# Gated linear attention with routed experts: late tiles routed in pairs, and each expert's weights split beside other products

## The chip, the cores and the metric

The kernel runs on one core of a Trainium2 chip, as one program. The metric is the time of an execution on the device in microseconds (us), as the median of three runs. Matrix products run on TensorE (PE), and the work around them on VectorE (DVE), ScalarE (ACT) and GpSimd (POOL); SyncE (SP) issues most of the DMA transfers. Each engine takes its instructions in the order of the program.

## The reference

Two layers follow one another. The first is a linear attention with a decay per key channel, for 4 batches of 8 heads with 768 positions and 48 channels a head. The second routes each of the 3072 rows (384 wide) to one of 8 experts, if a skip score is positive.

```python
for t in range(S):
    state = alpha[:, :, t, :, None] * state + einsum('bhd,bhe->bhde', k[:, :, t], v[:, :, t])
    y[:, :, t] = einsum('bhd,bhde->bhe', q[:, :, t], state)
x = y.transpose(0, 2, 1, 3).reshape(B * S, H * D)
do_compute = x @ w_skip > 0
xc = x[do_compute]
logits = xc @ w_gate
e_idx = argmax(logits)
gate_w = softmax(logits)[e_idx]
out = x
for e in range(8):                       # rows with e_idx == e
    h = maximum(xc[mask] @ w1[e], 0)     # 384 x 1024
    y[mask] = gate_w[mask] * (h @ w2[e]) # 1024 x 384
out[do_compute] = xc + y
```

## The kernel before

**Tiles.** The attention runs over 24 tiles of 128 positions; tile i is chunk i // 4 of batch i % 4, so four tiles in a row belong to four batches and the states are carried from each chunk to the next. One pass of the loop (iteration i) does different steps of several tiles: it loads tile i + 5, prepares decays of tile i + 3 (`decay_rev`, L252 to L259, and `decay_fwd`, L266 to L268, both on VectorE and GpSimd), computes `scores` and `causal` of tile i + 1 (L277 on PE, L284 on VectorE, writing `st`), then `inter`, `outer`, `carry` and `intra` of tile i, and `rows` and `logits` of tile i − 1. `rows` gives x of the tile (L369, L373), with the router's nine columns.

**Routing.** When the logits of a group of tiles are there, `route_expert` (a group) or `route_one` (a single tile) finds each row's expert, and writes a one-hot row `m` and a running count `cnt`. `route_rank` (L447 to L449) has PE add up the base, `cnt` and `m`, so each row gets its rank among the rows of its expert, and `route_slot` makes a slot number of it. The small instructions of the routing are taken a few at a time out of an iterator, at the points called `tick`. `scatter` then has GpSimd write each row's number and gate at its slot in a list `xs` in DRAM. Groups before: tiles 0 to 5, 6 to 11, 12 to 14, 15 to 17, and then each tile by itself.

**From tiles to experts.** Expert 0 takes the rows of tiles before 19 by a gather (`early_turn`, L500) and those of the last five (LATE = 19) by products with a one-hot matrix `hot` (`late_rows`, L494), whose operands are a high and a low part of x (`late_split`: high on ScalarE L507, low on GpSimd L508). Both land in the same sums, of which `first_turn` makes `xh0` and `xl0`.

**Experts.** Each of the 8 experts has 256 slots. Its products are exact to float32 by splitting every operand into a high part (a float32r copy) and a low part (the rest): three products a term. `up` has 4 groups of 18 products (L630), then ScalarE's `hh` (L634) and VectorE's `hl` (L635). `down` has two halves of 24 products (L646); VectorE's `o` (L649) follows each, and GpSimd scatters it to the output. Between the halves `turn` transposes the rows of the next expert (`xr`, gathered by GpSimd), with `xh` on ScalarE and `xl` on VectorE.

**Weights.** Each of w1 and w2 comes in 6 pieces of 512 columns (256 KB each), into 12 raw buffers. A split of a piece is a copy on ScalarE (L552, the high part) and a subtract on VectorE (L553, the low part). w1's piece q holds columns of row block q // 2, its even pieces the first half of the 1024 columns: group 0 of `up` needs pieces 0, 2 and 4. Before, w1 and w2 of expert e + 1 are split during expert e, two pieces beside each group of `up` and each half of `down`; of expert 0, eight pieces are split during tiles 20 to 23 and the other four during its first group. The order of the work is written out in `static_path`, and nothing is moved by a scheduler.

**Range check.** `guard` (L593, L597) loads alpha in 8 pieces of 576 KB, from ScalarE's queue, and has ScalarE pass over each twice (`over`): two passes behind the first half of `down` and one behind the second, until all 16 are done.

Of the kernel before, what the change touches and what calls it, by code (L numbers as in the profile page):

```python
# [10 lines left out]
F32 = mybir.dt.float32  # L11
F32R = mybir.dt.float32r
# [11 lines left out]
P = 128  # L24
# [30 lines left out]
class Kernel:  # L55
# [334 lines left out]
    def route_expert(self, g):  # L390
# [20 lines left out]
        for i in range(g0, g1):  # L411
            nc.gpsimd.tensor_tensor(self.cnt[:, i + 1, :], self.cnt[:, i, :], self.m[:, i, :], ALU.add)
# [39 lines left out]
    def route_slot(self, g):  # L452
# [16 lines left out]
        if g0 >= LATE:  # L469
            hot = self.late.tile([P, CAP], F32R, name=f"hot{g0}")  # L470
            yield nc.vector.tensor_scalar(out=hot, in0=self.slots0, scalar1=s2[:, 0, :], scalar2=None, op0=ALU.is_equal)
            self.work[g0]["hot"] = hot
# [30 lines left out]
    def late_split(self, i):  # L503
# [4 lines left out]
        nc.gpsimd.tensor_tensor(lo, w["x"], hi.bitcast(F32), ALU.subtract)  # L508
# [22 lines left out]
    def weight_pieces(self, e):  # L531

        self.wt[e] = {}
        for name, src in (("w1", self.w1), ("w2", self.w2)):
            raw = []
            self.wt[e][name] = [None, None, raw]
            for q in range(KT * F // PIECE):
                raw.append(self.wraw.tile([P, PIECE], F32, name="raw"))
                self.nc.sync.dma_start(out=raw[q], in_=src[e, :, q * PIECE:(q + 1) * PIECE])
                yield  # L540

    def split_pieces(self, e):

        nc = self.nc
        for name in ("w1", "w2"):
            pool = self.wpool[e % 2]
            hi = pool.tile([P, KT * F], F32R, name=name + "h")
            lo = pool.tile([P, KT * F], F32R, name=name + "l")
            self.wt[e][name][:2] = hi, lo
            for q, raw in enumerate(self.wt[e][name][2]):  # L550
                s = slice(q * PIECE, (q + 1) * PIECE)
                nc.scalar.copy(out=hi[:, s], in_=raw)  # L552
                nc.vector.tensor_tensor(lo[:, s], raw, hi[:, s].bitcast(F32), ALU.subtract)  # L553
                yield
# [246 lines left out]
    def static_path(self, ctx):  # L801
# [7 lines left out]
        groups = [(0, 6), (6, 12), (12, 15), (15, SOLO)] + [(g, g + 1) for g in range(SOLO, NT)]  # L809
# [7 lines left out]
        with ExitStack() as st:  # L817
# [20 lines left out]
            for i in range(NT):  # L838
# [204 lines left out]
```

## Time and profile before

| | |
|---|---|
| runs | 307.39, 308.74, 309.54 us; median 308.74 |
| profiled execution, its own time | 306.09 us |
| its span | 304.4 us |
| mean granted TensorE clock | 0.951 |
| PE, DVE, ACT, POOL busy | 278.6, 221.5, 163.2, 143.2 us |
| instructions | 7672 |
| first expert product | 148.66 us from the start of the span |

The profile shows one execution. A window of it, a stretch from A to B in us from the start of the span, lists how long each engine was busy, the clock that TensorE was granted (1.00 is full speed) and what the DMA engines moved. The chain of waits goes back from the last instruction to what released it, step by step. In a timeline a row is an instruction or several of the same kind in a row (x3), with its start and length; what stands in brackets at its end is how long the engine was idle before it, and what it had waited for. The line numbers are those of the kernel before; the changed kernel's are up to four lower from `weight_pieces` on.

### The profile page before, as it was taken

To read this page: it belongs to the slowest core of one execution; us is meant where nothing else is said; L and a number is where in the kernel's file an instruction comes from. 1 tells how busy PE (TensorE), PEld (TensorE's weight loads), DVE (VectorE), ACT (ScalarE), POOL (GpSimd) and SP (SyncE) were. 2 spreads that over 40 slices of the span, in tenths; PEclk is the share of its full clock that TensorE was granted. 3 is DMA by queue.
4 is the path that set the end of the run, shared out by engine and by line. 5 is a ranking of instruction groups with operands and counts; after the bars stand their busy time and mean duration, and the time that the engine had idled before them with its cause. 6 is when DMAs were issued, how large, how long until landed. Compare 5 with 4: busy or idle time off the path is not lost.

```text
span 304.4 us, 7672 instructions
## 1 busy us (share of the span) xinstructions
PE 278.6 (92%) x2862; PEld 259.1 (85%) x2862; DVE 221.5 (73%) x452; ACT 163.2 (54%) x374; POOL 143.2 (47%) x176
## 2 busy tenths in 40 slices
PE   8878999999999978976995989999999999999990
PEld 7667888888787866766994989999999999999990
DVE  8988979887789999788693467776767577676310
ACT  5336455556455353553473396959688685553300
POOL 8765656786877886728325311414022141402011
PEclk9999999999999995598798999999999999999996
DMA  7999999989899796043949978979968777510000
GB/s 238 316 237 222 240 226 258 199 160 205 135 219 211 224 134 208 26 132 89 327 121 381 371 219 255 283 247 281 310 187 289 233 253 241 195 35 20 18 23 25
DMA packets 31708, 60.80 MB, mean 200 GB/s; under 512 B 6590, under 2 KB 13545, under 8 KB 31664
## 3 DMA queue, kind: packets, MB, share of 16 engines
q1 hardware_dynamic: 26544, 50.44, 61.7%
q0 software_dynamic: 2944, 5.09, 5.4%
q10 hardware_dynamic: 2176, 4.72, 5.0%
q8 instruction: 24, 0.39, 0.6%
q14 instruction: 20, 0.16, 0.2%
HBM read 52.96 MB, written 8.89 MB: 203 GB/s over the span
## 4 chain that ended last, share of the span: by engine, by line
PE 73%; DMA 14%; DVE 5%; ACT 3%; issue 2%; POOL 1%; SPq 0%; POOLq 0%; DVEq 0%; ACTq 0%
PE ps_h L630 21%; PE ps_o L646 19%; PE ps_g L369 7%; PE ps_y L338 7%; PE ps_s L277 6%; DMA qka<-in_qka_dram 5%; PE ps_y L314 4%; DMA vt<-in_v_dram 3%; PE ps_v L324 2%; DMA xr<-out_dram,meta 2%; DMA alpha<-in_nat_dram 2%; PE ps_v L329 2%; PE ps_k L291 2%; PE ps_x L610 2%; DMA qka<-in_first_dram 1%
## 5 line engine op out<-in xcount | busy, mean ns | idle before, releaser
L651 POOL DMA_INDIRECT out_dram<-o,meta x16 | 16.9, 1059 | 100.5 <-DVE o L649 100.5
L646 PE MATMUL ps_o<-w2h,hh 128*128 128x384 f32 x128 | 44.4, 347 | 0.0
L646 PE MATMUL ps_o<-w2l,hh 128*128 128x384 f32 x128 | 43.7, 341 | 0.0
L646 PE MATMUL ps_o<-w2h,hl 128*128 128x384 f32 x128 | 43.7, 341 | 0.0
L268 POOL TENSOR_TENSOR qka<-qka,pfx 112x512 f32<-112x512 f32 x24 | 31.1, 1296 | 14.3 <-DVE seed L267 7.9
L553 DVE TENSOR_TENSOR w2l<-raw,w2h 128x512 fp32r<-128x512 f32 x48 | 31.3, 692 | 5.2 <-ACT w2h L552 5.2
L630 PE MATMUL ps_h<-xh,w1h 128*128 128x256 f32 x192 | 34.0, 284 | 0.8 <-DVE hl L635 0.8
L630 PE MATMUL ps_h<-xh,w1l 128*128 128x256 f32 x192 | 33.8, 283 | 0.0
L649 DVE SCALAR_TENSOR_TENSOR o<-ps_o,meta,xr 128x384 f32<-128x384 f32 x16 | 9.9, 618 | 32.7 <-PE ps_o L646 26.3
L630 PE MATMUL ps_h<-xl,w1h 128*128 128x256 f32 x192 | 33.2, 283 | 0.0
L277 PE MATMUL ps_s<-qka 48*128 48x128 f32 x384 | 28.9, 291 | 4.4 <-DVE st L284 2.0
L553 DVE TENSOR_TENSOR w1l<-raw,w1h 128x512 fp32r<-128x512 f32 x48 | 31.7, 699 | 1.3 <-ACT w1h L552 1.3
L635 DVE SCALAR_TENSOR_TENSOR hl<-ps_h,hh 128x512 fp32r<-128x512 f32 x32 | 22.0, 687 | 14.5 <-ACT hh L634 9.8
L259 POOL TENSOR_TENSOR qka<-qka,sfx 112x512 f32<-112x512 f32 x24 | 30.6, 1277 | 3.0 <-DVE sfx L252 2.4
L284 DVE COPY_PREDICATED st<-mask,ps_s 128x1024 f32<-128x1024 uint8 x24 | 31.5, 1311 | 0.5 <-PE ps_s L277 0.4
L277 PEld LDWEIGHTS ps_s<-qka 48*128 48x128 f32 x384 | 24.2, 193 | 7.9 <-POOL qka L268 2.6
L338 PE MATMUL ps_y<-st,vt 128*64 128x128 f32 (+1 forms) x384 | 30.3, 288 | 0.3 <-issue 0.2
L252 DVE TENSOR_TENSOR_SCAN sfx<-qka,seed 112x512 f32<-112x512 f32 x24 | 29.2, 1216 | 1.4 <-DMA qka<-in_qka_dram 1.0
L369 PEld LDWEIGHTS ps_g<-xw,xt 112*128 112x128 f32 x184 | 23.8, 202 | 7.0 <-issue 3.4
L369 PE MATMUL ps_g<-xw,xt 112*128 112x105 f32 x184 | 27.8, 297 | 1.9 <-DMA xw<-in_w_dram 1.9
L266 DVE TENSOR_TENSOR_SCAN pfx<-qka,seed 112x512 f32<-112x512 f32 x24 | 29.0, 1208 | 0.5
L634 ACT ACTIVATE hh<-ps_h 128x512 fp32r<-128x512 f32 x32 | 19.0, 595 | 19.0 <-PE ps_h L630 17.6
(146 smaller groups left out, 600.7 us busy)
## 6 DMA issues: line engine op xcount, KB each, us to landing
raw<-in_w_dram SPq DMA_DIRECT2D x96, 256.0 KB
qka<-in_qka_dram SPq DMA_DIRECT2D x36, 288.0 KB
vt<-in_v_dram SPq DMA_DIRECT2D x24, 192.0 KB
out_dram<-x SPq DMA_DIRECT2D x24, 192.0 KB
alpha<-in_nat_dram ACTq DMA_DIRECT2D x8, 576.0 KB
qka<-in_first_dram SPq DMA_DIRECT2D x4, 672.0 KB
out_dram<-xr SPq DMA_DIRECT2D x5, 192.0 KB
qka<-in_first_dram SPq DMA_DIRECT2D x2, 448.0 KB
```

Source lines behind the costliest of these rows:

```text
L252: nc.vector.tensor_tensor_scan(flat(sfx)[:, ::-1], w["qka"][:PD, 2 * SW + 1:QW + 1][:, ::-1], flat(self.seed)[:, ::-1], 0.0, ALU.mult, ALU ...
L259: nc.gpsimd.tensor_tensor(w["kh"][:PD], w["kh"][:PD], sfx[:PD], ALU.mult)
L266: nc.vector.tensor_tensor_scan(flat(pfx), w["qka"][:PD, 2 * SW:QW], flat(self.seed), 0.0, ALU.mult, ALU.max)
L268: nc.gpsimd.tensor_tensor(w["qh"][:PD], w["qh"][:PD], pfx[:PD], ALU.mult)
L277: nc.tensor.matmul(ps[:, h, p * P:(p + 1) * P], lhsT=kh[r, p, :], rhs=qh[r, p, :], start=True, stop=True)
L284: self.nc.vector.copy_predicated(w["st"], self.mask, w["ps"])
L338: nc.tensor.matmul(y, lhsT=w["v"][:, o:o + m], rhs=w["st"][:, h, p * P:(p + 1) * P], start=(i < B and a == 0), stop=(a == NP // 2 - 1))
L369: nc.tensor.matmul(pg[:, p, :], lhsT=w["xt"][:PD, p, :], rhs=self.xw[:PD, p, :], start=True, stop=True)
L553: nc.vector.tensor_tensor(lo[:, s], raw, hi[:, s].bitcast(F32), ALU.subtract)
L630: nc.tensor.matmul(ps[:, u, :], lhsT=a[:, k, f * P:(f + 1) * P], rhs=b[:, k, :], start=(n == 0), stop=(n == len(order) - 1))
L635: nc.vector.scalar_tensor_tensor(out=hl, in0=ps, scalar=0.0, in1=hh.bitcast(F32), op0=ALU.max, op1=ALU.subtract)
L646: nc.tensor.matmul(ps, lhsT=a[:, f, js], rhs=b[:, f, :], start=(n == 0), stop=(n == 3 * FT - 1))
```

## The change

Five things are different.

- The last tiles are routed in the groups 18; 19 and 20; 21 and 22; 23. For a group that begins after tile 11, `cnt` is added up on VectorE and not on GpSimd. The routing of tiles 15 to 17 is spread over iteration 19, three steps at a tick.
- `late_split` has its low part on VectorE.
- w1 of expert 0 is loaded at iterations 6, 8 to 16, and split at 7, 9 to 17; w2 of expert 0 is loaded at iterations 18 and 19.
- w2 of every expert is split beside its own `up`, two pieces behind each of the first three groups, and w1 of the next expert beside `down`, three pieces behind each half (two and four in expert 0). Loads follow the same order, and w1 of expert 1 is loaded behind the two lists of slots.
- The last tile's `inter` and `intra` stand behind the loop; the scatters of tiles 21 and 22 come ahead of the rank of tile 23.

```diff
@@ route_expert
         for i in range(g0, g1):
-            nc.gpsimd.tensor_tensor(self.cnt[:, i + 1, :], self.cnt[:, i, :], self.m[:, i, :], ALU.add)
+            eng.tensor_tensor(self.cnt[:, i + 1, :], self.cnt[:, i, :], self.m[:, i, :], ALU.add)
@@ route_slot
-        if g0 >= LATE:
-            hot = self.late.tile([P, CAP], F32R, name=f"hot{g0}")
...
+        for i in range(max(g0, LATE), g1):
+            self.work[i]["hot"] = hot = self.late.tile([P, CAP], F32R, name=f"hot{i}")
...
@@ late_split
-        nc.gpsimd.tensor_tensor(lo, w["x"], hi.bitcast(F32), ALU.subtract)
+        nc.vector.tensor_tensor(lo, w["x"], hi.bitcast(F32), ALU.subtract)
@@
+    def weight_pieces(self, e, name):
+        raw = []
+        self.wt.setdefault(e, {})[name] = [None, None, raw]
+        for q in range(KT * F // PIECE):
+            raw.append(self.wraw.tile([P, PIECE], F32, name="raw"))
+            self.nc.sync.dma_start(out=raw[q], in_=getattr(self, name)[e, :, q * PIECE:(q + 1) * PIECE])
+            yield
+
+    def split_pieces(self, e, name):
+
+        nc = self.nc
+        pool = self.wpool[e % 2]
+        hi = pool.tile([P, KT * F], F32R, name=name + "h")
+        lo = pool.tile([P, KT * F], F32R, name=name + "l")
+        self.wt[e][name][:2] = hi, lo
+        for q, raw in enumerate(self.wt[e][name][2]):
+            s = slice(q * PIECE, (q + 1) * PIECE)
+            nc.scalar.copy(out=hi[:, s], in_=raw)
+            nc.vector.tensor_tensor(lo[:, s], raw, hi[:, s].bitcast(F32), ALU.subtract)
+            yield
@@ static_path, the loop over tiles
-        groups = [(0, 6), (6, 12), (12, 15), (15, SOLO)] + [(g, g + 1) for g in range(SOLO, NT)]
+        groups = [(0, 6), (6, 12), (12, 15), (15, SOLO), (SOLO, 19), (19, 21), (21, 23), (23, NT)]
...
-                    fetch = self.weight_pieces(0)
-                advance(fetch, {18: 3, 19: 3, 22: 3, 23: 3}.get(i, 0))
+                    fetch = self.weight_pieces(0, "w2")
+                if i == 6:
+                    fetch = self.weight_pieces(0, "w1")
+                advance(fetch, 1 - i % 2 if i < NT - 6 else 3)
...
-                if i == 20:
-                    split = self.split_pieces(0)
+                if i == 7:
+                    split = self.split_pieces(0, "w1")
...
+                many = 3 if i in (SOLO, SOLO + 1) else 1
...
-                advance(split, 1)
+                advance(split, i % 2)
@@ behind the loop over tiles
-            fetch = self.weight_pieces(1)
-            advance(fetch, 6)
-            a, b = NT - 2, NT - 1
+            a, b = NT - 3, NT - 1
+            self.inter(b)
+            self.intra(b)
...
+            for i in after + [a, b - 1]:
+                self.scatter(i)
             self.route_rank((b, NT))
...
@@ the loop over experts
+            fetch = self.weight_pieces(1, "w1")
+            advance(fetch, 6)
+            check = self.guard()
             for e in range(E):
-                more = self.split_pieces(e + 1) if e + 1 < E else iter(())
-                if e == 0:
-                    check = self.guard()
+                split = self.split_pieces(e, "w2")
+                fetch = self.weight_pieces(e + 1, "w2") if e + 1 < E else iter(())
...
-                        advance(split, 12)
-                        advance(fetch, 6)
-                        split, fetch = more, self.weight_pieces(2)
-                    else:
-                        if g == 0:
-                            split, fetch = more, self.weight_pieces(e + 2) if e + 2 < E else iter(())
-                        advance(split, 3 if e == 0 else 2)
-                        advance(fetch, 3 if e == 0 else 2)
+                    advance(split, 2)
+                    advance(fetch, 2)
+                split = self.split_pieces(e + 1, "w1") if e + 1 < E else iter(())
+                fetch = self.weight_pieces(e + 2, "w1") if e + 2 < E else iter(())
                 for j in range(NB):
                     self.down(e, j)
                     if j == 0 and e + 1 < E:
                         self.turn(e + 1)
-                    advance(split, 2)
-                    advance(fetch, 2)
+                    n = 3 if e else (2, 4)[j]
+                    advance(split, n)
+                    advance(fetch, n)
                     advance(check, 2 - j)
```

Three places show how the instructions stand now. The first is VectorE at the end of expert 1, from its last group of `up` to the first group of expert 2; a row names the operation, the tile written and those read, and the number of instructions. Before:

```order
L635 SCALAR_TENSOR_TENSOR hl<-ps_h,hh 128x512
L553 TENSOR_TENSOR w2l<-raw,w2h 128x512 x2
L649 SCALAR_TENSOR_TENSOR o<-ps_o,meta_2381,xr_2374 128x384
L613 TENSOR_TENSOR xl<-ps_x,xh 128x3x128 x2
L553 TENSOR_TENSOR w2l<-raw,w2h 128x512 x2
L649 SCALAR_TENSOR_TENSOR o<-ps_o,meta_2381,xr_2374 128x384
L553 TENSOR_TENSOR w2l<-raw,w2h 128x512 x2
L635 SCALAR_TENSOR_TENSOR hl<-ps_h,hh 128x512
L553 TENSOR_TENSOR w1l<-raw,w1h 128x512 x2
```

And now:

```order
L631 SCALAR_TENSOR_TENSOR hl<-ps_h,hh 128x512
L645 SCALAR_TENSOR_TENSOR o<-ps_o,meta_2315,xr_2308 128x384
L609 TENSOR_TENSOR xl<-ps_x,xh 128x3x128 x2
L549 TENSOR_TENSOR w1l<-raw,w1h 128x512 x3
L645 SCALAR_TENSOR_TENSOR o<-ps_o,meta_2315,xr_2308 128x384
L549 TENSOR_TENSOR w1l<-raw,w1h 128x512 x3
L631 SCALAR_TENSOR_TENSOR hl<-ps_h,hh 128x512
L549 TENSOR_TENSOR w2l<-raw,w2h 128x512 x2
```

Three subtracts of w1 of the next expert (pieces 3, 4 and 5) now stand behind the second `o`, where subtracts of w2 of the next expert stood.

The second place is ScalarE behind the first half of `down` of expert 0. Now:

```order
L608 CAST xh<-ps_x 128x3x128 x2
L548 CAST w1h<-raw 128x512 x2
L589 DMA alpha<-in_nat_dram 128x2x576 x2
L593 ACTIVATE over,odd<-alpha,lim 128x1152 x2
L548 CAST w1h<-raw 128x512 x4
L589 DMA alpha<-in_nat_dram 128x2x576
L593 ACTIVATE over,odd<-alpha,lim 128x1152
L630 ACTIVATE hh<-ps_h 128x512
```

The four copies that stand behind the two passes of the range check are w1 of expert 1; before, copies of its w2 stood there.

The third place is VectorE at iteration 19, where tiles 15 to 17 are routed (`mx` to `cnt`, `sl`), with `st` of `causal` and `sfx` and `pfx` of the decays of tile 22. Before:

```order
L400 TENSOR_REDUCE mx_1771<-logit_202 128x3
L402 TENSOR_TENSOR d_1773<-logit_202,mx_1771 128x24
L403 TENSOR_TENSOR eq_1772<-logit_202,mx_1771 128x24
...
L409 SCALAR_TENSOR_TENSOR m_205<-logit_202,eq_1772 128x24
...
L252 SCALAR_TENSOR_TENSOR sfx_1798<-qka4_127,seed_132 112x512
...
L284 COPY_PREDICATED st0_144<-mask_69,ps_s_1804 128x1024
L266 SCALAR_TENSOR_TENSOR pfx_1814<-qka4_127,seed_132 112x512
...
L465 TENSOR_TENSOR sl_1858<-ps_g_1848,m_205 128x24
```

And now:

```order
L252 SCALAR_TENSOR_TENSOR sfx_1804<-qka4_127,seed_132 112x512
...
L400 TENSOR_REDUCE mx_1806<-logit_202 128x3
...
L402 TENSOR_TENSOR d_1808<-logit_202,mx_1806 128x24
L403 TENSOR_TENSOR eq_1807<-logit_202,mx_1806 128x24
...
L284 COPY_PREDICATED st0_144<-mask_69,ps_s_1821 128x1024
...
L409 SCALAR_TENSOR_TENSOR m_205<-logit_202,eq_1807 128x24
L266 SCALAR_TENSOR_TENSOR pfx_1834<-qka4_127,seed_132 112x512
...
L412 TENSOR_TENSOR cnt_203<-cnt_203,m_205 128x8 x3
...
L465 TENSOR_TENSOR sl_1884<-ps_g_1874,m_205 128x24
```

The routing's first steps stood ahead of `sfx` and are now behind it and between `st` and `pfx`; `cnt`, on which the rank of PE waits, is now VectorE's and stands behind `pfx`.

More of the change, by code (lines that the diff above doesn't have):

```diff
@@ L869, in static_path @@
                     self.decay_fwd(i + 3)
[L870 to L886 removed]
+                    self.tick(many)
+                if i < NT - 1:
+                    self.inter(i)
+                    if ranked:
+                        self.tick(99)
+                    if ranked and late:
+                        self.route_rank(ranked)
+                        self.small = self.route_slot(ranked)
+                        self.tick(99)
+                    self.outer(i)
+                    self.carry(i)
+                    self.intra(i)
+                if i > 0:
                     self.rows(i - 1, None if late else ranked)
```

98 lines of the change are left out of this document (29 added, 69 removed).

## The prediction

> **What bounds the kernel now.** I read the page first, then the chain of waits, then sums over windows stage by stage, then the timelines at the places that the change touches. From the page:
>
> ```profile
> span 304.4 us, 7672 instructions
> PE 278.6 (92%) x2862; PEld 259.1 (85%) x2862; DVE 221.5 (73%) x452; ACT 163.2 (54%) x374; POOL 143.2 (47%) x176
> PEclk9999999999999995598798999999999999999996
> ```
>
> TensorE is busy for 92% of the span, so every gap that the change opens on PE costs its full length; and PE's clock falls in two places, near slices 16 to 19 (the last tiles) and near 21 to 22 (expert 0). The sums over windows give the stages: tiles in steady state, the last tiles up to the first expert product, two short pieces at their start, a piece of expert 0, and experts 1 to 7. The columns are length, busy time and count of each engine, granted clock, DMA share and GB/s.
>
> ```profile
> 40.40:105.30 64.90, 64.57 (x1038) 55.36 (x1038) 55.57 (x109) 34.74 (x105) 49.20 (x71) 1.00 0.95 209
> 106.60:148.40 41.80, 34.72 (x355) 29.98 (x355) 33.93 (x120) 17.93 (x53) 28.91 (x31) 0.76 0.54 136
> 110.00:112.00 2.00, 1.49 (x14) 1.08 (x10) 1.90 (x7) 0.00 (x0) 1.60 (x4) 1.00 1.00 26
> 112.00:114.00 2.00, 0.94 (x14) 0.84 (x15) 2.00 (x2) 1.79 (x7) 1.69 (x4) 1.00 0.53 87
> 118.00:120.00 2.00, 2.00 (x16) 1.67 (x11) 1.97 (x4) 0.58 (x1) 1.57 (x3) 0.50 0.33 89
> 166.00:172.00 6.00, 6.00 (x29) 6.00 (x30) 2.75 (x5) 1.51 (x3) 1.03 (x1) 0.76 1.05 382
> 181.50:296.60 115.10, 115.06 (x808) 114.36 (x806) 73.84 (x127) 71.14 (x132) 24.64 (x23) 1.00 0.61 193
> ```
>
> From 181.50 on PE is busy 115.06 of 115.10 us: nothing is to be won there, only lost. The chain of waits shows the experts, each 72 up products, 24 down products, the next expert's transposes and 24 down products more:
>
> ```profile
> 148.66 8.66 PE ps_h L630 x72
> 190.76 8.63 PE ps_h L630 x72
> 208.48 8.55 PE ps_h L630 x72
> 217.03 4.23 PE ps_o L646 x24
> 221.26 0.65 PE ps_x L610 x6
> 221.91 4.22 PE ps_o L646 x24
> 226.13 8.64 PE ps_h L630 x72
> ```
>
> An expert takes 226.13 − 208.48 = 17.65 us, one up product 8.55 / 72 = 0.119. Experts 0 and 1 together took 190.76 − 148.66 = 42.10, which is 6.8 over two undisturbed ones.
>
> **The change part by part.**
>
> *A. Expert 0's w1 is split during tiles 7 to 17.* Six splits of one ACT copy and one DVE subtract come in, and six loads go past on SP's queue. DVE is busy 55.57 of 64.90 us there, so 9.3 us are free for 6 × 0.69 = 4.1 (the duration is in the next fence). PE's own work hides them: 0, at most +2 if the copies delay a state.
>
> *B. The last tiles (106.6 to 148.4).* PE is busy 34.72 of 41.80 at a clock of 0.76. The chain there runs through splits and two DVE instructions of the routing:
>
> ```profile
> 128.72 0.53 ACT w1h L552
> 129.27 0.69 DVE w1l L553
> 133.59 0.53 ACT w1h L552
> 134.13 0.69 DVE w1l L553
> 136.04 0.53 ACT w2h L552
> 136.59 1.07 DVE w2l L553
> 138.30 0.60 DVE w2l L553
> 141.20 1.12 DVE on L426
> 142.98 1.57 DVE m L432
> ```
>
> All these splits leave the stage: 0.53 + 0.69 + 0.53 + 0.69 + 0.53 + 1.07 + 0.60 = 4.6 off the chain. `on` and `m` are stretched while a GpSimd subtract of the late rows runs (1.12 and 1.57 against 0.08 and 0.24 for the same lines earlier in this chain, at 130.04 and 130.54, as the next fence shows). With the subtract on VectorE that goes: 1.04 + 1.33 = 2.4 off. These waits come on PE for the routing (the first two rows are the short `on` and `m`):
>
> ```profile
> 130.04 0.08 DVE on L426
> 130.54 0.24 DVE m L432
> 112.11 0.17 PE L448 MATMUL ps_g<-cnt,one_b 128*128 128x24 bf16 x1 [0.49 <-POOL cnt L412]
> 116.81 0.17 PE L449 MATMUL ps_v<-m,tri 128*128 128x8 bf16 x1 [1.14 <-DVE m L431]
> ```
>
> Pairs remove two of the five ranks inside the loop; at about 1 us each (0.49 to 1.14) that is 2 off. Added: five subtracts on VectorE, bounded by 0.60 to 0.69 (a split's subtract of 512 columns; these have 384) though part lies beside PE, so +1.5 to 2; and the rank of tiles 15 to 17 now waits for `cnt` on VectorE behind `st` and `pfx` of iteration 19, about 2.5 us in place of 0.49, so +2. The rank that waits holds `outer`, `carry` and `intra` behind it in PE's order. Sum −4.6 − 2.4 − 2 + 2 + 2 = −5. Ends: −1 if the removed links were only masking each other, −9.5 if the second stretch of low clock goes too. The first should stay: PE is busy 1.49 + 0.94 of 4 us at 110 to 114 and the clock is 0.50 afterwards, and the longer rank wait lies just there.
>
> *C. Expert 0.* What can go is the 6.8 above. Where it was lost:
>
> ```profile
> 163.21 0.55 PE L610 MATMUL ps_x<-ident,xr 128*128 128x128 f32 x3 [1.60 <-DMA xr<-out_dram,meta]
> 165.84 0.90 PE L610 MATMUL ps_x<-ident,xr 128*128 128x128 f32 x3 [2.08 <-DMA xr<-out_dram,meta]
> 166.79 6.65 DMA alpha<-in_nat_dram
> ```
>
> Rows of expert 1 that came late (1.60 + 2.08), the low clock behind them, and `hh` standing behind the range check that waited for alpha. Fewer weights are in flight now, so I take all 6.8 off. What comes in: behind the first half of down, ACT's order is two casts of xh, two w1h copies, two alpha loads, two range checks, then four w1h copies. The first group of expert 1 needs w1 pieces 0, 2 and 4. The rows of the same work at another expert, and two rows of VectorE:
>
> ```profile
> 221.62 0.86 ACT L612 CAST xh<-ps_x 128x384 fp32r<-128x384 f32 x2 [2.93 <-PE ps_x L610]
> 222.37 1.15 ACT L552 CAST w2h<-raw 128x512 fp32r<-128x512 f32 x2
> 223.41 1.27 ACT L597 ACTIVATE over<-alpha,lim 128x1152 bf16<-128x1152 f32 x1
> 225.22 1.26 ACT L597 ACTIVATE over<-alpha,lim 128x1152 bf16<-128x1152 f32 x1 [0.45 <-ACT over L597]
> 226.47 1.13 ACT L552 CAST w2h<-raw 128x512 fp32r<-128x512 f32 x2
> 226.17 0.62 DVE L649 SCALAR_TENSOR_TENSOR o<-ps_o,meta,xr 128x384 f32<-128x384 f32 x1 [1.81 <-PE ps_o L646]
> 227.11 1.29 DVE L553 TENSOR_TENSOR w2l<-raw,w2h 128x512 fp32r<-128x512 f32 x2 [0.32 <-ACT w2h L552]
> ```
>
> Counted from the end of the first down half (221.26 in these rows): alpha is issued at +2.2, and lands between 1.5 us later (576 KB at the 382 GB/s of the window from 166 on) and 6.65 (the row, under full queues); I take the middle, 4.1, so +6.3. Two checks of 1.3 give +8.9, the copies of pieces 2, 3 and 4 at 0.53 +10.5, the last subtract +11.2. PE is ready at 0.65 + 4.22 and five products (0.6), +5.5. So a stall of 5.8 (3.1 to 8.3), and a low clock after it. One such stretch cost about 1.4: 0.76 over 6 us. In sum −6.8 + 5.8 + 1.4 = +0.4, ends −3 and +4.
>
> *D. The six boundaries into experts 2 to 7.* Before, w1 of the next expert was split during up and only w2 stood here, which nobody needs for 8 us. Now VectorE's order is `o` (which waits for the last down product), then w1l of pieces 3, 4 and 5, and PE needs piece 4 at its sixth product. Without range checks in between: 0.62 + 2 × 0.645 (half of 1.29) − 0.6 = 1.3 a boundary. With two checks ahead of copies 3 to 5 ACT is later: copies of three pieces end 0.53 after the two shown (at about 224.0), two checks take 2.6 or, with an alpha load between them, 3.0 (1.27, 0.45, 1.26), two copies 1.06, the subtract 0.69, so piece 4 is ready at 228.4 or 228.8 where PE would want it at 226.13 + 0.6. That is 1.7 or 2.1, with 0.1 at each of two hand-overs 1.9 or 2.3. The checks fill experts 1 to 4, two of each kind; experts 5 and 6 have none that bind. Sum 2 × 2.3 + 2 × 1.9 + 2 × 1.3 = 11.0, ends 8 and 13 (a tenth of a us to half a us either way in each). No work covers it: PE has only these products in order.
>
> *E. The clock.* Between 110 and 114 PE was idle for 0.51 + 1.06 us, in more than one gap (one is the 0.49 at 112.11), and the clock was 0.50 at 118 to 120; after the gaps of 1.60 and 2.08 in expert 0 it was 0.76 over 6 us. So a 2-us gap can cost 0.24 × 6 = 1.4. I expect it at three of the six boundaries: +4, ends 0 and +8. The Trainium skill ("TensorE: Matmul & The Clock Gate", HAM oscillation) has a drop only after PE idles for more than about 3.4 us. By that rule this term is 0 and the sum 4 lower; the gaps of 1.57 us together before the clock of 0.50 speak against it.
>
> Sum: 0 − 5 + 0.4 + 11.0 + 4 = +10.4. The profiled execution took 306.09 by its own time (span 304.4), so 316.5; the median of the runs is 308.74, 2.65 above it, and I set the sum on the median: 319.
>
> **The rivals.**
>
> *R1, faster.* The boundaries don't stall, because the DVE has pieces 3 to 5 done in time (w1l taken ahead of `o`, or the copies early enough that 0.6 us suffice). Then D and E are 0, and C loses its stall: −5 − 6.8 = −12, 297. For it: DVE is busy only 73.84 of 115.10 us in the experts. Against it: the row at 226.17, where `o` starts only once PE has finished, and what stands behind it can't start sooner. Where C keeps its stall (−5 + 0.4 = −4.6), a boundary may cost at most (4.6 − 3.1) / 6 = 0.25 us for the kernel to come out faster by 1%, and 0.77 us leaves the time as it was.
>
> *R2, no change to measure.* The last tiles keep their clock (B = −9.5), and the boundaries cost D alone (E = 0): −9.5 + 0.4 + 11 = +2, 311. For it: the waits removed lie where the clock is low. Against it: the new wait for `cnt` at the start of that stretch.
>
> *R3, much slower.* The clock falls at every boundary (6 × 1.4 = 8.4), alpha lands late (+4), and the late tiles gain nothing but their splits less the new waits (−3): 11 + 8.4 + 4 − 3 = +20, 329. For it: every boundary leaves PE idle about as long as one gap of expert 0. Against it: the products of 8.6 us around each boundary keep PE full.
>
> **How the numbers follow.** Forecast 0.61, R3 0.15, R2 0.13, R1 0.11. About 1%, 3.1 us, is what a measurement of this kernel can tell from no change. R1 is faster (0.11), R2 within (0.13), the forecast and R3 slower (0.76). The range goes from 309.5 (it holds R2 and the low ends of B and E together) to 326.5 (the upper ends of C and D, half of R3); left out are R1 and the other half of R3, 0.19.
>
> **What would show it.** D: at the start of each expert from 2 on PE idle for 1.3 to 2.3 us, ended by DVE's w1l, and `o` just ahead of it on DVE. C: PE waiting at expert 1 for w1, ACT's idle time before it ended by alpha. B: the first expert product near 143 to 145 instead of 148.66, `on` and `m` short, a wait of 2 us or more at the rank of tiles 15 to 17. E: digits under 9 on the PEclk line after slice 24. Wrong I am if PE shows no idle time at the boundaries, or if the first expert product comes before 140.

## The result, and the profile after

The changed kernel takes 341.43 us (median of 4 runs, 337.19 to 342.24) against 308.99 us before: 1.103 times as long, with a 95% interval of 1.093 to 1.113. The forecast was 319, up to 326.5. The direction was right; the size was not. Executions more than 1.5% above the fastest of the same kernel count in no ratio and in no stage below (tick_back has too few others for a ratio, and lag_less_step and dve_at_once have no stages), but in the medians.

The page of the changed kernel:

```profile
span 340.0 us, 7648 instructions
PE 293.3 (86%) x2856; PEld 270.8 (80%) x2856; DVE 222.1 (65%) x445; ACT 163.4 (48%) x368; POOL 134.1 (39%) x165
PEclk9987999599975997595799789999997999999998
```

PE's share of the span fell from 92% to 86%, and the clock now falls in many places, most of them in the first half, where it was full before. To see the stages, both traces are cut at the same points of the program: the start of tile 7's `scores` (up to there both programs issue the same work, but for one load), the `scores` 11 tiles later, and the first expert product. The columns are length, busy time and count of each engine, granted clock, DMA share and GB/s. Before:

```profile
0.00:40.33 40.33, 34.47 (x459) 30.72 (x459) 35.58 (x62) 19.26 (x49) 27.95 (x42) 1.00 0.99 246
40.33:96.49 56.16, 55.83 (x887) 47.84 (x887) 46.99 (x89) 30.69 (x92) 41.76 (x61) 1.00 0.96 206
96.49:148.50 52.01, 44.71 (x515) 38.58 (x515) 43.91 (x141) 22.36 (x68) 37.58 (x42) 0.80 0.59 150
148.50:304.40 155.90, 143.57 (x1006) 141.98 (x1004) 95.06 (x162) 90.83 (x167) 35.91 (x32) 0.97 0.62 202
```

After:

```profile
0.00:44.69 44.69, 38.27 (x459) 34.15 (x459) 35.71 (x62) 19.32 (x49) 27.92 (x42) 0.92 0.99 238
44.69:115.47 70.78, 62.08 (x887) 53.47 (x887) 48.15 (x94) 33.23 (x98) 41.62 (x61) 0.88 0.83 173
115.47:169.90 54.43, 44.30 (x508) 38.44 (x508) 40.71 (x126) 18.43 (x55) 30.30 (x31) 0.81 0.50 111
169.90:340.00 170.10, 148.67 (x1004) 144.73 (x1004) 97.49 (x164) 92.47 (x169) 34.29 (x32) 0.96 0.57 187
```

The 35.6 us between the spans are +4.4 up to tile 7, +14.6 in the eleven tiles behind it, +2.4 in the last tiles and +14.2 in the experts. The first 4.4 can't be put down to the change: among all the kernels below that point lies between 39.7 and 44.7, and the instructions up to it are the same but for that load. In the middle stage DVE is busy for 1.2 us more (48.15 against 46.99), but the stage is 14.6 longer.

**Where the tiles wait.** The timeline at iteration 8, where tiles 0 to 5 are ranked. What stands in brackets is the idle time of the engine before the row:

```profile
56.10 0.60 ACT L548 CAST w1h<-raw 128x512 fp32r<-128x512 f32 x1
56.74 0.69 DVE L549 TENSOR_TENSOR w1l<-raw,w1h 128x512 fp32r<-128x512 f32 x1 [1.31 <-ACT w1h L548]
57.34 1.21 DVE L252 TENSOR_TENSOR_SCAN sfx<-qka,seed 112x512 f32<-112x512 f32 x1
58.48 0.18 DVE L409 SCALAR_TENSOR_TENSOR m<-logit,eq 128x48 bf16<-128x48 f32 x1
58.71 0.20 POOL L258 TENSOR_TENSOR total<-a,sfx 112x4 f32<-112x4 f32 x1 [2.58 <-DVE m L409]
60.09 1.59 POOL L412 TENSOR_TENSOR cnt<-cnt,m 128x8 bf16<-128x8 bf16 x6
61.46 0.20 PE L448 MATMUL ps_g<-cnt,one_b 128*128 128x48 bf16 x1 [2.20 <-POOL cnt L412]
...
92.45 0.24 ACT L404 ACTIVATE ex<-d 128x48 f32<-128x48 f32 x1 [5.50 <-POOL d L402]
100.38 0.20 PE L448 MATMUL ps_g<-cnt,one_b 128*128 128x48 bf16 x1 [3.37 <-POOL cnt L412]
```

VectorE, idle for 1.31 us with `sfx` next in its order, waits for ScalarE's copy of a weight that nobody needs for another 100 us. `m`, ahead of `sfx` before, stands behind it now; GpSimd waits for both, adds up `cnt` only after its decay, and PE stands at the rank for 2.20 us. Tiles 6 to 11 repeat it with 3.37 us (the last row), and there ScalarE, too, waited 5.50 us for GpSimd. In the kernel before, `m` came just ahead of `sfx` (which began at 51.23), and PE did not wait at the rank:

```profile
51.10 0.21 DVE L409 SCALAR_TENSOR_TENSOR m<-logit,eq 128x48 bf16<-128x48 f32 x1
54.74 0.18 PE L448 MATMUL ps_g<-cnt,one_b 128*128 128x48 bf16 x1
```

The chain shows what follows the 2.20 us, a half clock (0.50 granted from 61.4 to 66; 16 `scores` products took 1.09 before):

```profile
62.54 2.01 PE ps_s L277 x16
```

**Where the experts wait.** The chain at the starts of `down`, one row an expert from 1 to 7, with the first wait for alpha, the low clock in expert 1 and one of three rows that name a raw weight:

```profile
184.62 4.20 DMA alpha<-in_nat_dram
193.16 10.68 PE ps_h L626 x70
203.84 4.23 PE ps_o L642 x24
211.20 3.85 DMA raw<-in_w_dram
224.01 4.22 PE ps_o L642 x24
243.76 4.22 PE ps_o L642 x24
265.45 4.22 PE ps_o L642 x24
285.19 4.22 PE ps_o L642 x24
304.74 4.23 PE ps_o L642 x24
323.95 8.46 PE ps_o L642 x48
```

From one start of `down` to the next it is 20.17, 19.75, 21.69, 19.74, 19.55 and 19.21 us, where an expert took 17.65. PE's timeline shows the waits into experts 1, 2, 3 and 4:

```profile
192.12 0.58 PE L626 MATMUL ps_h<-xh,w1h 128*128 128x256 f32 x1 [3.49 <-ACT over L593]
193.16 0.58 PE L626 MATMUL ps_h<-xh,w1h 128*128 128x256 f32 x1 [0.46 <-ACT w1h L548]
214.98 0.39 PE L626 MATMUL ps_h<-xh,w1h 128*128 128x256 f32 x1 [1.80 <-ACT w1h L548]
215.79 0.39 PE L626 MATMUL ps_h<-xh,w1l 128*128 128x256 f32 x1 [0.19 <-DVE w1l L549]
234.73 0.39 PE L626 MATMUL ps_h<-xh,w1h 128*128 128x256 f32 x1 [1.38 <-ACT w1h L548]
254.89 0.39 PE L626 MATMUL ps_h<-xh,w1h 128*128 128x256 f32 x1 [1.80 <-ACT w1h L548]
```

### The profile page after: what moved, and what is told of

It is laid out like the page before. It is cut to its first block, busy times and chain, and to the rows that moved or that the text cites. A ratio compares the mean times of both kernels' runs of the same rounds, so it can differ in the third digit from the quotient of the medians.

```text
span 340.0 us, 7648 instructions
## 1 busy us (share of the span) xinstructions
PE 293.3 (86%) x2856; PEld 270.8 (80%) x2856; DVE 222.1 (65%) x445; ACT 163.4 (48%) x368; POOL 134.1 (39%) x165
## 4 chain that ended last, share of the span: by engine, by line
PE 51%; DMA 20%; DVE 11%; ACT 8%; issue 4%; POOL 3%; SPq 1%; POOLq 0%; ACTq 0%; DVEq 0%
PE ps_h L626 21%; PE ps_o L642 12%; DMA qka<-in_qka_dram 9%; PE ps_s L277 4%; DMA vt<-in_v_dram 4%; DVE sfx L252 3%; PE ps_y L338 3%; DMA raw<-in_w_dram 3%; PE ps_g L369 3%; ACT w1h L548 3%; DVE w1l L549 2%; PE ps_y L314 2%; DMA qka<-in_first_dram 2%; POOL qka L259 2%; ACT over L593 2%
## 5 line engine op out<-in xcount | busy, mean ns | idle before, releaser
L626 PE MATMUL ps_h<-xh,w1h 128*128 128x256 f32 x192 | 37.4, 296 | 10.9 <-ACT w1h L548 6.8
L626 PEld LDWEIGHTS ps_h<-xh,w1h 128*128 128x128 f32 x192 | 29.8, 198 | 12.9 <-ACT w1h L548 8.2
L626 PE MATMUL ps_h<-xh,w1l 128*128 128x256 f32 x192 | 36.8, 293 | 3.1 <-DVE w1l L549 2.7
L277 PE MATMUL ps_s<-qka 48*128 48x128 f32 x384 | 31.6, 310 | 6.5 <-POOL total L258 1.8
L277 PEld LDWEIGHTS ps_s<-qka 48*128 48x128 f32 x384 | 26.8, 210 | 10.4 <-POOL qka L268 2.9
L626 PE MATMUL ps_h<-xl,w1h 128*128 128x256 f32 x192 | 34.4, 290 | 0.0
L626 PEld LDWEIGHTS ps_h<-xh,w1l 128*128 128x128 f32 x192 | 29.2, 196 | 4.5 <-DVE w1l L549 3.8
L338 PE MATMUL ps_y<-st,vt 128*64 128x128 f32 (+1 forms) x384 | 32.6, 310 | 0.0
L369 PE MATMUL ps_g<-xw,xt 112*128 112x105 f32 x184 | 29.2, 307 | 3.2 <-DMA xw<-in_w_dram 2.4
L369 PEld LDWEIGHTS ps_g<-xw,xt 112*128 112x128 f32 x184 | 25.1, 211 | 7.9 <-issue 3.9
```

What stands on the lines that cost most here:

```text
L277: nc.tensor.matmul(ps[:, h, p * P:(p + 1) * P], lhsT=kh[r, p, :], rhs=qh[r, p, :], start=True, stop=True)
L338: nc.tensor.matmul(y, lhsT=w["v"][:, o:o + m], rhs=w["st"][:, h, p * P:(p + 1) * P], start=(i < B and a == 0), stop=(a == NP // 2 - 1))
L369: nc.tensor.matmul(pg[:, p, :], lhsT=w["xt"][:PD, p, :], rhs=self.xw[:PD, p, :], start=True, stop=True)
L626: nc.tensor.matmul(ps[:, u, :], lhsT=a[:, k, f * P:(f + 1) * P], rhs=b[:, k, :], start=(n == 0), stop=(n == len(order) - 1))
```

## The experiments

The experts' waits were as forecast; the tiles' were not. Two things there could make the routing late. One stands in the diff of the two kernels, in lines that the excerpt ahead of the prediction leaves out, and was overlooked: the call `self.tick(1 ...)` behind a tile's `rows` moved under the condition `if ranked and not late`, so that an iteration takes five steps of the routing and not six. **Theory T** puts the tiles' loss on this lost step. **Rival S** puts it on the splits, whose subtract ties VectorE to ScalarE. For the experts, **theory P** is that w1's needed pieces come last, and **rival R** that the raw weights land late, since the chain names their transfers at three boundaries.

In the table the tiles' stage runs from tile 7's `scores` to the first expert product, with its first part, the eleven tiles up to tile 18's `scores`, in a column of its own; the experts' runs from there to the end of the span. All are of the one profiled execution of each kernel. In the changed kernel, tick_back, even_first and tick_even, which have the same last tiles, the part behind the eleven took from 51.8 to 54.6 us, so a difference of less than 3 us there proves little by itself. Medians are compared with the kernel before on the same chip (309.0, 309.3, 308.1 and 310.3 in the four groups).

| kernel | median | ratio to before (95%) | tiles | of these, the eleven | experts |
|---|---|---|---|---|---|
| before | 308.99 |  | 108.2 | 56.2 | 155.9 |
| changed | 341.43 | 1.103 (1.093–1.113) | 125.2 | 70.8 | 170.1 |
| tick_back | 330.53 |  | 114.8 | 60.2 | 172.3 |
| splits_late | 325.62 | 1.058 (1.050–1.066) | 112.8 | 56.4 | 169.9 |
| even_first | 315.67 | 1.023 (1.016–1.030) | 121.0 | 68.4 | 151.6 |
| tick_even | 308.71 | 0.999 (0.995–1.003) | 115.1 | 63.3 | 151.3 |
| before_less_step | 312.62 | 1.009 (1.005–1.014) | 111.2 | 57.2 | 155.1 |
| lag_split | 304.93 | 0.985 (0.981–0.989) | 109.3 | 55.3 | 151.1 |
| tick_even_late | 309.28 | 0.998 (0.994–1.003) | 113.3 | 56.4 | 150.7 |
| tiles_before | 304.86 | 0.985 (0.981–0.988) | 107.4 | 56.0 | 153.5 |
| lag_cnt | 300.17 | 0.976 (0.967–0.984) | 104.1 | 55.3 | 151.3 |
| lag_less_step | 301.76 | 0.980 (0.970–0.989) |  |  |  |
| lag_singles | 304.09 | 0.985 (0.974–0.995) | 107.0 | 55.3 | 152.5 |
| cnt_at_once | 300.94 | 0.974 (0.969–0.980) | 104.5 | 55.3 | 151.2 |
| dve_at_once | 303.24 | 0.975 (0.968–0.982) |  |  |  |

### The step of the routing back: tick_back

```diff
                     if ranked and not late:
                         self.small = chain(self.small, self.route_slot(ranked))
-                        self.tick(1 if i - 2 < SOLO - 1 else 99)
+                    self.tick(1 if i - 2 < SOLO - 1 else 99)
```

> Changed kernel, with the one step of the routing taken again in every iteration behind the tile's rows (the change had put that call under the condition that a group is ranked, so an iteration takes five steps, not six). Everything else as changed. Theory T (lost step): cnt of the groups (0,6) and (6,12) comes a step late and PE's rank waits for it (2.20 and 3.37 us, each with a low clock behind it); with the step back both waits go, tiles 10 to 18 take about 40 us as before, and the kernel takes 325 to 330 in place of 341. Rival S (splits in the tiles): VectorE's w1l waits for ScalarE's copy ahead of sfx, and that alone makes it late; then the waits stay and the time is 337 or more.

Measured 330.53, half a us above T's range (the four runs go from 324.03 to 332.58): PE's waits at both ranks are gone, and the tiles take 114.8 in place of 125.2. But 6.6 us over the kernel before stay, 4.1 of them in the eleven tiles, which T had back at their old length.

### Expert 0's w1 split late: splits_late

```diff
-                if i == 7:
+                if i == SOLO:
                     split = self.split_pieces(0, "w1")
...
-                advance(split, i % 2)
+                advance(split, 1)
```

> Changed kernel, with expert 0's w1 split at iterations 18 to 23 instead of 7 to 17; its loads stay where the change put them. Theory T: the waits at the ranks of (0,6) and (6,12) stay, and some 3 to 5 us are added among the last tiles: 341 to 346. Rival S: the waits go, some 10 to 14 us less among tiles 10 to 18, 3 to 5 more among the last: 330 to 335.

Measured 325.62, lower than either theory had it. The tiles take 112.8 with the step still lost, and the eleven tiles 56.4, as before. So removing either one alone removes most of the loss of the eleven tiles, but only moving the splits removes all of it: T and S are each a part of the answer.

### w1's even pieces first: even_first

```diff
-        for q in range(KT * F // PIECE):
+        for q in (0, 2, 4, 1, 3, 5) if name == "w1" else range(6):
...
-        for q, raw in enumerate(self.wt[e][name][2]):
+        for n, raw in enumerate(self.wt[e][name][2]):
+            q = (0, 2, 4, 1, 3, 5)[n] if name == "w1" else n
...
-                    n = 3 if e else (2, 4)[j]
+                    n = 3
```

> Changed kernel, with w1's pieces loaded and split in the order 0, 2, 4, 1, 3, 5, and three behind each half of down in expert 0 as well. The pieces that the first group of up needs then stand ahead of the range check on ScalarE and ahead of the second o on VectorE. Theory P (order of the pieces): the waits at the boundaries (about 2 us each, and 4 into expert 1) and the low clock behind two of them go; experts 0 to 7 take 13 to 18 us less: 323 to 328. Rival R (the raw weights land late, as the chain of waits names them at three boundaries): the waits stay at about their length, 336 to 342.

Measured 315.67, below the range of P, and the experts take 151.6 in place of 170.1. The chain of this kernel:

```profile
202.70 8.63 PE ps_h L627 x72
211.33 4.21 PE ps_o L643 x24
215.54 0.65 PE ps_x L607 x6
216.20 4.22 PE ps_o L643 x24
220.42 8.64 PE ps_h L627 x72
```

An expert takes 220.42 − 202.70 = 17.72 again. The amount of weights is the same and so are the queues; with the order of six pieces changed, the waits are gone. The edit also lets the needed pieces land earlier, so by itself it doesn't part P from R. ScalarE in the changed kernel does, here into expert 2:

```profile
212.55 1.26 ACT L593 ACTIVATE over<-alpha,lim 128x1152 bf16<-128x1152 f32 x1 [0.45 <-ACT over L593]
213.80 1.64 ACT L548 CAST w1h<-raw 128x512 fp32r<-128x512 f32 x3
```

The copies of the needed pieces begin as soon as the checks are done, without a wait for a transfer; at the other boundaries, too, they follow without a wait on what stands ahead of them on ScalarE. R falls: the transfers that the chain named there were not what PE waited for. Of the 23.9 us between the two spans, 18.5 are the experts', 4.2 the tiles' and 1.2 lie ahead of tile 7.

### Both: tick_even

Both edits above in one kernel.

> Changed kernel with both: the step of the routing back in every iteration, and w1's pieces in the order 0, 2, 4, 1, 3, 5. Theories T and P together: about 341 - 13 - 16 = 312, 306 to 316, near the kernel before at 309. If either of them is wrong, 323 or more.

Measured 308.71, as expected, and no different from before. The tiles still take 115.1, 6.9 more than before, all of it in the eleven tiles (63.3 against 56.2), and the experts 4.6 less. So with the step back, and no wait at the two ranks, the splits alone still cost these tiles 7 us (4 in tick_back).

### The lost step alone: before_less_step

```diff
 (kernel before)
-                    self.tick(1 if i - 2 < SOLO - 1 else 99)
+                    if i - 2 >= SOLO - 1 or (ranked and not late):
+                        self.tick(1 if i - 2 < SOLO - 1 else 99)
```

> Kernel before, with one edit: the step of the routing behind the tile's rows is taken only where a group is ranked (five steps an iteration, as in the changed kernel). Theory T (lost step): the ranks of (0,6) and (6,12) wait for cnt as in the changed kernel, 2 to 3.4 us each and a low clock behind them: 315 to 320. Rival S (the splits among the tiles are what makes VectorE late, and the step matters only together with them): 308 to 311.

Measured 312.62, between the two: the tiles take 3.0 more, 1.1 of it in the eleven. The rows of the same iteration show why so little:

```profile
54.84 0.18 DVE L409 SCALAR_TENSOR_TENSOR m<-logit,eq 128x48 bf16<-128x48 f32 x1
57.81 0.18 PE L448 MATMUL ps_g<-cnt,one_b 128*128 128x48 bf16 x1 [0.20 <-DMA qka<-in_qka_dram]
```

`m` stands behind `sfx` here too, but VectorE is early enough, and PE waits 0.20 us, not 2.20. The step was slack: it is lost without much harm as long as nothing else uses that slack.

### The subtract one iteration behind its copy: lag_split

The kernel tick_even, with one more edit, in the split of expert 0's w1 alone:

```diff
             nc.scalar.copy(out=hi[:, s], in_=raw)
+            if e == 0 and name == "w1":
+                yield
             nc.vector.tensor_tensor(lo[:, s], raw, hi[:, s].bitcast(F32), ALU.subtract)
...
-                advance(split, i % 2)
+                advance(split, 1)
```

> The kernel with both repairs (step back, even pieces first; 308.7), in which VectorE's subtract of expert 0's w1 stands one iteration behind ScalarE's copy of the piece. Same instructions, same numbers on each engine. If VectorE is late because it waits for that copy (theory S1): tiles 6 to 18 return to about 5.0 us each, 299 to 304. If it is late because of the work itself (theory S2, 0.69 us more in an iteration whose groups fill VectorE): 307 to 311.

Measured 304.93, between the two but nearer to S1. The windows of the eleven tiles in tick_even and in lag_split:

```profile
40.89:104.22 63.33, 58.46 (x887) 50.45 (x887) 47.99 (x94) 33.18 (x98) 42.68 (x61) 0.95 0.92 204
40.86:96.15 55.29, 54.85 (x887) 47.66 (x887) 50.01 (x93) 32.22 (x95) 41.69 (x60) 1.00 1.02 235
```

The eleven tiles take 55.29 at full clock (56.16 before), with the splits among them and DVE busier than in either (50.01). The same instructions, one iteration apart, cost nothing there: the work is hidden, and the wait for ScalarE was the harm. What is left of the loss lies behind 96.15, 54.1 us against 52.0 before.

### No splits among the tiles, step back: tick_even_late

The kernel tick_even, with the edit of splits_late.

> The kernel with both repairs, and with expert 0's w1 split at iterations 18 to 23 as in the kernel before, and not among tiles 7 to 17. Theory S1 or S2: tiles 6 to 18 as before, some 8 us less there, 4 more among the last tiles: 303 to 306. If the splits among the tiles cost nothing once the step is back: 311 to 314.

Measured 309.28, between the expectations: the tiles take 113.3, with neither of the two causes in tiles 7 to 17, and the eleven tiles 56.4. The rank of tiles 15 to 17 in its timeline:

```profile
119.60 0.18 PE L448 MATMUL ps_g<-cnt,one_b 128*128 128x24 bf16 x1 [6.04 <-DVE cnt L412]
```

PE waits 6.04 us there, so the last tiles have a loss of their own, a part of which is the splits that stand among them here.

### The tiles of before, the experts of after: tiles_before

The whole loop and tail of the kernel before, with expert 0's w1 alone split at iterations 20 to 23; the experts as in even_first.

> All 24 tiles and the tail as in the kernel before (groups, count on GpSimd, low part of late x on GpSimd, w1 of expert 0 split at iterations 20 to 23), the experts as in the changed kernel with w1's even pieces first. If the order of weights in the experts is worth what it takes out of experts 0 and 1 (6.8 us of waits before) and nothing comes back at the boundaries: 300 to 303, faster than both kernels. If the late alpha still holds expert 1: 305 to 308.

Measured 304.86, between the two. The experts take 2.4 less than before (153.5), not 4.6. Its timeline shows what holds expert 1, the rows that came late in the kernel before too:

```profile
165.74 0.55 PE L607 MATMUL ps_x<-ident,xr 128*128 128x128 f32 x3 [2.22 <-DMA xr<-out_dram,meta]
```

In lag_singles, which also has single late tiles, this wait is 1.96, and in tick_even 0.22. So that wait goes with how the last tiles are routed, not with the order of the weights. The reason that the second expectation gave, alpha landing late, isn't what this row shows.

### cnt on GpSimd, the step lost again, single tiles: lag_cnt, lag_less_step, lag_singles

The first two are lag_split with one edit each; the third is tiles_before with the early loads and the lagged splits of lag_split.

```diff
 (lag_cnt)
-            eng.tensor_tensor(self.cnt[:, i + 1, :], self.cnt[:, i, :], self.m[:, i, :], ALU.add)
+            (nc.gpsimd if g1 <= SOLO else nc.vector).tensor_tensor(self.cnt[:, i + 1, :], self.cnt[:, i, :], self.m[:, i, :], ALU.add)
```

> The kernel with step back, even pieces first and the lagged subtract (304.9), with cnt of the groups (12,15) and (15,18) on GpSimd again as in the kernel before; the pairs keep VectorE. If the waits of PE at cnt and behind it (2.17 at iteration 17, 3.81 at the rank of (15,18)) come from cnt standing behind sfx, st and pfx on VectorE: 4 to 6 us less among the last tiles, 299 to 301. If GpSimd is as late there: 304 to 306.

> The same kernel (304.9) with the step of the routing lost again. If step and splits made the tiles late together (each alone 5 to 6 us, both 21), the lagged subtract takes the harm out and the lost step costs what it costs the kernel before, 3 to 6 us: 308 to 311. If the lost step is enough by itself in this order: 315 to 320.

> The kernel with the tiles of the kernel before (single late tiles, cnt of (12,15) and (15,18) and low part of late x on GpSimd) and the experts with even pieces first, with expert 0's w1 split in the lagged way among tiles 7 to 18 and not among the last four. The splits' 3 us on the chain of the last tiles go: first expert product near 145 in place of 149.7, 300 to 302. If pairs are worth the 5 us that I gave the last tiles, lag_cnt is faster than this by 1 us or more; if not, this one is.

lag_cnt: 300.17, as the first theory had it, and the tiles take 104.1, 5.2 less than in lag_split. But only 1.3 of that lie between the `scores` of tiles 18 and 23, where this `cnt` stands. The other 4.0 lie behind, where ScalarE, and VectorE with it, stood idle in lag_split's profiled execution until 2.4 us after the rank of tiles 21 and 22 was done, for a reason that the profile doesn't name ("remote"):

```profile
143.56 0.58 ACT L341 COPY xt<-ps_y 112x512 f32<-112x512 f32 x1 [3.47 <-remote]
```

The intervals of the two (0.981 to 0.989 and 0.967 to 0.984) overlap as well, so what `cnt` on VectorE costs isn't proved by this pair.

lag_less_step: 301.76, faster than either expectation; its interval and lag_split's overlap, so with the lagged subtract the lost step costs nothing that can be seen. This settles the question between T and S: the wait for the copy does the harm (63.3 against 55.3 in the eleven tiles), and the lost step, which costs them 1.1 without the splits, makes it about twice as large (68.4 and 70.8) by taking away the slack of `m`.

lag_singles: 304.09, slower than expected; its tiles take 2.9 more than lag_cnt's, but the two intervals (0.974 to 0.995 and 0.967 to 0.984) overlap. So the pairs (with the low part on VectorE) look worth about 3 us in the profiles, and the times don't prove it. Against tiles_before, lag_singles tells what w1's splits cost the last tiles when these are routed singly: nothing that can be seen (51.4 us behind the eleven tiles with them and 51.7 without; both ratios are 0.985).

### The routing of tiles 15 to 17 at once: cnt_at_once, dve_at_once

From lag_cnt and from lag_split:

```diff
-                    if i - 1 >= SOLO:
+                    if i - 1 >= SOLO - 1:
                         self.tick(99)
```

> The kernel lag_cnt (300.2), with tiles 15 to 17 routed all at once at the end of iteration 18, as in the kernel before, and not a few steps at a time through iteration 19. If the wait of 5.26 us at their rank in lag_cnt comes from the spread routing (m stands behind st on VectorE): the wait is under 1 us, and the time 296 to 298. If not: 299 to 301.

> The same routing at once, with cnt of the groups (12,15) and (15,18) on VectorE as the change has it (so lag_split, 304.9, with this one edit). If the spread alone made the rank of tiles 15 to 17 late: 299 to 301, the wait there under 1 us, and the 2.17 us at iteration 17 behind cnt of (12,15) stays. If the place of cnt on VectorE is what holds PE: 303 to 306.

cnt_at_once: 300.94, no gain over lag_cnt, though the wait at that rank went from 5.26 to 1.30 us. In lag_cnt and in cnt_at_once, the rank of tiles 15 to 17:

```profile
119.96 0.18 PE L448 MATMUL ps_g<-cnt,one_b 128*128 128x24 bf16 x1 [5.26 <-DMA raw<-in_w_dram]
```

```profile
114.51 0.17 PE L448 MATMUL ps_g<-cnt,one_b 128*128 128x24 bf16 x1 [1.30 <-POOL cnt L412]
```

And yet the stage is 104.1 in the one and 104.5 in the other: what PE did not lose there it lost in the tiles that follow. That the last tiles run at the pace of VectorE's and ScalarE's small steps, so that a wait of PE moves rather than goes, would explain it; it was not tested. dve_at_once: 303.24, in the range for "cnt on VectorE holds PE", but its ratio, 0.975, is that of cnt_at_once (0.974), and its runs go from 299.38 to 304.88, so it decides nothing. Only cnt_at_once lies clear of lag_split (0.969 to 0.980 against 0.981 to 0.989): `cnt` on GpSimd and the routing at once are worth something together, and their shares stay open.

lag_cnt and cnt_at_once beat both kernels, by 2.4% and 2.6% of the kernel before.

## Why the prediction was right and wrong

**The experts (C, D, E): right in mechanism, and in the sum with some luck.** Forecast +0.4 + 11 + 4 = 15.4; measured 14.2. D came out larger than its term and E smaller, which nearly cancels.

*C.* Alpha landed 4.20 us after its issue; the 4.1 taken was the middle of 1.5 to 6.65, so that was luck. PE's wait into expert 1 was 3.49 + 0.46 = 4.0, not 5.8. The low clock behind it cost 2.3 (10.68 for 70 products, against 70 × 0.119 = 8.3), not 1.4. Together 6.3 for 7.2. From the first product of expert 0 to that of expert 2 it is 42.85 us, where it was 42.10: +0.75 for +0.4.

*D.* Forecast 2.3, 1.9, 2.3, 1.9, 1.3, 1.3; the steps less 17.65 are 2.52, 2.10, 4.04, 2.09, 1.90, 1.56. The alternation of the two kinds with and without an alpha load between the checks is there (idle 1.80, 1.38, 1.80). The last two are 0.3 to 0.6 over the term. At the others PE stood after two products, at ScalarE's copy of piece 4 behind the checks; the subtract, which the forecast's sign named, ended only a short wait behind that (0.19 at 215.79).

*E.* One low clock, not three: into expert 4, in the step of 4.04. So E was about 1.5 instead of 4, D about 12.7 instead of 11.

**Step A (splits of expert 0's w1 among tiles): wrong, and with the lost step it is most of the miss.** Where the forecast had 0, the eleven tiles lost 14.6 us. The prediction took 0, at most +2, from VectorE's free time in the window (9.3 us) against the work (4.1). The work did fit: lag_split shows it. What failed is the sentence "PE's own work hides them". It asked how long the instructions take, not what the first of them waits for. A subtract that needs ScalarE's copy, placed ahead of `sfx` on an engine that goes in order, holds up `sfx` until ScalarE has come to the end of the iteration before. What stands behind a wait, and who waits for that, was asked of the rank at iteration 19 and of the boundaries, and not here.

**A step that the prediction lacked: the lost step of the routing.** The diff shows the call's indentation change; the prediction took the loop's ticks as unchanged but for the three steps at a time of iteration 19. Alone it costs 3.0 us in the tiles (before_less_step); with the splits it raises them from 115 to between 121 and 125. None of the signs that the prediction named, of being right or wrong, looked at these tiles.

**Step B (the last tiles, −5): wrong.** In the changed kernel the stage took 2.4 us more, and in the three others with the same last tiles it took 54.6, 52.5 and 51.8, against 52.0: between −0.2 and +2.6. The term for the new rank wait was about right: 2.5 forecast, and 2.93 measured, as the first row below shows. The term of −4.6, for the splits that leave the chain, was not a saving of that size: single late tiles took as long without w1's splits (51.7) as with them (51.4), as if the removed links had only masked others, which was the prediction's own end of −1. In the paired kernel their place matters more, by about 3 us (57.0 in tick_even_late, 54.1 in lag_split, with ratios that lie clear of each other). And VectorE's two-input instructions are stretched anew while GpSimd works on `qka`, just as `on` and `m` were. The changed kernel's rows:

```profile
136.86 0.18 PE L448 MATMUL ps_g<-cnt,one_b 128*128 128x24 bf16 x1 [2.93 <-DVE cnt L412]
132.08 1.95 DVE L408 TENSOR_TENSOR eq<-eq,m 128x24 f32<-128x24 f32 x1
135.62 1.39 DVE L412 TENSOR_TENSOR cnt<-cnt,m 128x8 bf16<-128x8 bf16 x2
132.71 1.28 POOL L259 TENSOR_TENSOR qka<-qka,sfx 112x512 f32<-112x512 f32 x1
135.53 1.26 POOL L268 TENSOR_TENSOR qka<-qka,pfx 112x512 f32<-112x512 f32 x1 [1.54 <-DVE pfx L266]
```

`eq` ends at 134.03, just behind GpSimd's `qka` (133.99), and PE's wait for `cnt` at 136.86, just behind the next one (136.79). That fits the Trainium skill ("SBUF — State Buffer", SBUF: two separate sides), by which a VectorE operation with two inputs in SBUF and a GpSimd operation that reads SBUF can't use their shared port at once. The prediction counted that collision where it left (2.4), not where the change made it anew. What it costs the time isn't shown. With `cnt` of tiles 12 to 17 back on GpSimd the stage is 48.8 and 49.2 (lag_cnt and cnt_at_once), so −3.2 and −2.8 of the −5 are there, in kernels other than the one changed.

**The rivals.** R1 fell with the waits at the boundaries, R2 with the last tiles, which gained nothing; R3 (329) put its extra time on the clock at the boundaries, on alpha and on the last tiles, so it came nearer to the time for reasons that mostly weren't so. No rival looked at tiles 6 to 17, which lost 14.6 us.

## What to carry to other kernels

Work that fits into an engine's idle time is free only if nothing it waits for comes later than what stands behind it: with the second half of each split a full step behind the first, the same work cost these tiles nothing. When a transfer or a split is moved next to its use, see which piece the first consumer needs, and take that one first; here an order of six pieces was worth 18.5 us. In a diff that moves code, read the indentation of the calls that pace other work: slack is lost there without a trace, until something else needs it.

## What the runs showed of the hardware

A gap of 2.20 us on PE was enough for a half clock behind it (16 products in 2.01 us, not 1.09), and of the four boundaries with gaps of 1.4 to 1.8 us, those into experts 2 to 5, one brought a low clock. So neither the forecast's "three of six" nor the rule of more than about 3.4 us that it quoted describes these gaps. The Trainium skill ("TensorE: Matmul & The Clock Gate", Part 1) says that the window in which the activity is measured runs freely; that would fit a gap that counts or not by where it falls, but no run here tests it.

The chain of waits can name a transfer that PE did not wait for: at three boundaries it went through raw weights (3.85, 3.30 and 2.33 us in the changed kernel), while ScalarE, which reads them, began its copies without waiting for them, and a new order of the same transfers and splits ended the waits.

The first 40 us, the same instructions in all kernels but for one load, took from 39.7 to 44.7 us in the profiled executions. Stages are better compared from a common point of the program than from the start of the span.
